# Two linear-attention and feed-forward layers on one core: down weights loaded behind small memsets, and a new order of the work

## The chip, the cores and the metric

The kernel runs on one core of a Trainium2 chip. The metric is device time in microseconds (us) of one execution; less is better. A core has five engines with an instruction queue each: TensorE (PE, matrix products), VectorE (DVE), ScalarE (ACT), GpSimd (POOL) and SyncE (SP, which here issues nearly all transfers). They run side by side and wait for each other by semaphores. Transfers are carried out by 16 DMA engines.

## The reference

x has 2048 rows of 512 columns. Two layers, one after the other, are applied twice, with the same weights:

```python
x = x + A(layernorm(x))      # 32 heads of 16, 4 segments of 512 rows
x = x + B(layernorm(x))      # gelu(x @ w_gate) * (x @ w_up) @ w_down, 1792 wide
# A, for segment s of a head:
p = softmax(q @ k.T * scale + causal_mask)         # within the segment
a_mem = (phi(q) @ M) / (phi(q) @ z + 1e-6)         # memory of earlier segments
o = g * a_mem + (1 - g) * (p @ v);  M += phi(k).T @ v;  z += sum(phi(k))
# phi(t) = t + 1 where t > 0, else exp(t); the result is o @ wo
```

## The kernel before

The work is cut into eight pieces, k = 0 to 7: four segments of 512 rows in the first pass through the two layers, four in the second. For each, PE makes q and k (512 rows by 128 columns at a time, four products of 128 deep each), v, the scores (computed transposed, so keys lie on partitions), the products of the exponentials (`pt`) with v, the memory's update and its reading, the output product, then gate, up and down of the feed-forward layer. All weights stay in on-chip memory: `wg_sb` and `wu_sb` (4 tiles of 1792 columns) and `wd_sb` (14 tiles of 512).

Nearly all products are split in four: four matmuls with 32 output columns of the array each, which run side by side (`product`, L654). So one product of 512 columns is four weight loads and four matmuls, eight instructions. PE's queue has 27,448 instructions.

The order of the work on every engine is set by a planner that runs when the program is built. `Clocks` keeps a modelled time for PE and for each other engine; work that becomes ready is posted to an engine (`post`, L255) with the time from which it is ready and a slack, and `serve` (L271) hands out the job with the earliest ready time plus slack. PE's products are items with a due time; at each step the main loop (at the end of the program) takes a step of scores if its exponentials have room, else the next ready item by due time. If there is no ready item but scores are still to come, it emits an unread product: a product of the constant tile `warm` into a free bank that nobody reads. The plan decides the order only; on the chip each engine works through its queue in that order and waits for real events. The table `CHANGES` alters the planner's slacks and due times each 8 us of modelled time.

ACT computes the exponentials (L1491), gelu (L1273) and some copies out of the accumulators; POOL masks the diagonal blocks of `pt` (L1464, `affine_select`) and makes `kS`, masked keys (L816); DVE does the rest. SP issues the weight loads (L498), the DMA transposes of normed rows and of phi(k) (L611: `xnT<-xn`, `phik<-e`), the copies of the odd heads' keys (L844: `kB<-kf`) and of half-segments' values (L888: `vS<-vaug`).

Weight loads are posted to SP from a list `pieces` of name, modelled time, size and a function that issues the load. The seven loads of the down weights (256 KB each) are the last of it: the first at `WD` = 40.3 us, then one each `WD_GAP` = 1.39 us. They have nothing to wait for but their place in SP's queue and the semaphores that DMA transfers share. The third part of x (`X3`, 512 KB) is such a piece too. At the start, PE runs `WARM` = 15 products of the whole array on the constant tile while the first rows of x are loaded and normed.

## Time and profile before

| | us |
|---|---|
| median of three runs | 557.79 (553.35 to 559.0) |
| the profiled execution | 553.77 |
| its span, first to last instruction | 552.0 |
| PE busy in it | 540.5 |
| mean granted clock of PE | 0.996 of full |

The profile is of one execution. The page gives busy times and groups of instructions; further views, which the prediction quotes, are the busy time by stretch (one row for each stretch of time; for each engine busy us and number of instructions, then the clock that PE was granted, the DMA engines' busy share and the GB/s that they moved), the waits (engine and line that waited, what it waited for, total us, number, longest), and the timeline (start, duration, engine, line, instruction, number merged into the row, and in brackets the idle time before it and what ended it). "issue" stands for idle time with no event that the profile shows. Durations of products overlap, since PE is pipelined: the step from one product to the next is shorter than the duration of one.

### The profile page before, as it was taken

Reading aid. Unit: us, or ns where it says so; the run is one execution under the profiler, and the core shown is the slowest. Engines: PE = TensorE matmul, PEld = TensorE weight load, DVE = VectorE, ACT = ScalarE, POOL = GpSimd, SP = SyncE. Lnnn points to the kernel's source line nnn. Section 1 sums busy time; section 2 is a strip of 40 time slices with the busy share of each in tenths; the row PEclk is TensorE's granted clock in tenths of the full one; section 3 lists DMA queues with packets and bytes.
Section 4 is the critical chain, followed back from the end, with each engine's and each line's share of the span. In section 5 each row is a group of like instructions: output and inputs, shape, how many; then the busy total and the mean of one; then the engine's idle time right before and its main releaser. Section 6 shows DMA issues by size and latency. Waiting matters only on the chain.

```text
span 552.0 us, 29935 instructions
## 1 busy us (share of the span) xinstructions
PE 540.5 (98%) x13723; PEld 296.2 (54%) x13723; DVE 434.6 (79%) x832; ACT 417.5 (76%) x391; POOL 242.2 (44%) x432
## 2 busy tenths in 40 slices
PE   8999899999999999999999999999999999999997
PEld 4446764765445444545444444555455455545994
DVE  7999599768996988689896976488989797587162
ACT  3899688989999877977989778947888865950600
POOL 6469044257538333924483345148593333121000
PEclk9999899999999999999999999999999999999999
DMA  8758515202500233301414020212254004100001
GB/s 254 188 130 173 127 34 98 34 4 55 96 13 4 37 48 60 51 2 33 60 33 60 14 41 4 50 33 41 42 89 71 4 8 94 13 12 32 14 5 41
DMA packets 69775, 30.39 MB, mean 55 GB/s; under 512 B 55120, under 2 KB 69200, under 8 KB 69648
## 3 DMA queue, kind: packets, MB, share of 16 engines
q1 hardware_dynamic: 69504, 28.46, 26.8%
q8 instruction: 107, 1.75, 1.4%
q14 instruction: 20, 0.16, 0.1%
q10 hardware_dynamic: 144, 0.01, 0.0%
HBM read 9.71 MB, written 2.10 MB: 21 GB/s over the span
## 4 chain that ended last, share of the span: by engine, by line
PE 89%; DVE 5%; ACT 2%; issue 1%; DMA 1%; POOL 0%; ACTq 0%; SPq 0%; DVEq 0%
PE big L654 75%; PE big L1421 8%; PE big L1117 6%; ACT pt L1491 1%; DVE x_sb L1218 1%; DVE st L677 1%; DMA vS<-vaug 1%; DVE byq L1145 1%; DMA x_sb<-in_A_x_dram 1%; DVE xn L713 0%; DVE st L1505 0%; POOL rs L1509 0%; DVE e L948 0%; DVE kS L816 0%; DVE ab L1153 0%
## 5 line engine op out<-in xcount | busy, mean ns | idle before, releaser
L1491 ACT ACTIVATE pt<-big 128x2048 bf16<-128x2048 f32 (+1 forms) x158 | 273.5, 1740 | 74.1 <-PE big L1421 68.1
L1464 POOL TENSOR_SCALAR_AFFINE_SELECT pt<-pt 64x256 bf16<-64x256 bf16 (+4 forms) x318 | 157.3, 522 | 227.1 <-ACT pt L1491 225.7
L1308 DVE TENSOR_TENSOR gel<-gel,big 128x512 bf16<-128x512 bf16 x112 | 74.9, 681 | 42.3 <-PE big L654 34.8
L654 PE MATMUL big<-xnT,wu_sb 128*32 128x512 bf16 (+1 forms) x2240 | 106.4, 339 | 0.5 <-issue 0.5
L654 PE MATMUL big<-xnT,wg_sb 128*32 128x512 bf16 (+1 forms) x2240 | 106.0, 337 | 0.0
L654 PE MATMUL big<-wd_sb,gel 128*32 128x512 bf16 (+2 forms) x1848 | 105.7, 373 | 0.0
L654 PEld LDWEIGHTS <-wu_sb 128*32 128x32 bf16 x2240 | 58.4, 97 | 35.1 <-issue 4.6
L654 PEld LDWEIGHTS <-wg_sb 128*32 128x32 bf16 x2240 | 57.9, 97 | 34.9 <-issue 5.4
L654 PEld LDWEIGHTS <-gel 128*32 128x32 bf16 x1848 | 46.7, 97 | 43.6 <-issue 4.6
L1218 DVE TENSOR_TENSOR x_sb<-x_sb,big 128x512 bf16<-128x512 bf16 (+1 forms) x65 | 43.1, 667 | 29.5 <-PE big L654 29.4
L1145 DVE STREAM_TRANSPOSE byq<-big 128x512 f32<-128x512 f32 x64 | 45.1, 705 | 12.5 <-PE big L1117 12.0
L1117 PE MATMUL big<-pt,vaug 128*32 128x64 bf16 (+5 forms) x1152 | 45.0, 263 | 2.4 <-issue 2.4
L677 DVE BATCH_NORM_STATS2 st<-x_sb 128x6 f32<-128x512 bf16 x60 | 40.5, 675 | 0.5
L1273 ACT ACTIVATE gel<-big 128x512 bf16<-128x512 f32 x64 | 34.9, 604 | 3.9 <-PE big L654 3.9
L654 PE MATMUL big<-xnT,wq_sb 128*32 128x512 bf16 (+1 forms) x528 | 35.0, 374 | 0.2 <-DVE xnT L755 0.2
L654 PE MATMUL big<-xnT,wk_sb 128*32 128x512 bf16 (+2 forms) x528 | 34.4, 373 | 0.2
L654 PE MATMUL big<-wv_sb,xnT 128*32 128x512 bf16 x512 | 32.3, 380 | 0.0
L654 PE MATMUL big<-wo_sb,aT 128*32 128x512 bf16 x512 | 31.9, 380 | 0.0
L816 POOL TENSOR_SCALAR kS<-kf,maskA 128x256 bf16<-128x256 bf16 x28 | 29.2, 1043 | 3.9 <-PE big L1421 3.0
L713 DVE TENSOR_SCALAR xn<-x_sb,mv,rs 128x512 bf16<-128x512 bf16 x64 | 28.9, 499 | 1.7 <-POOL rs L1509 0.9
L1117 PE MATMUL big<-pt,vS 128*32 128x64 bf16 x960 | 28.4, 193 | 1.3 <-DMA vS<-vaug 1.3
L816 POOL TENSOR_SCALAR kS<-kf,maskB 128x256 bf16<-128x256 bf16 x28 | 29.5, 1054 | 0.3
(98 smaller groups left out, 644.0 us busy)
## 6 DMA issues: line engine op xcount, KB each, us to landing
vS<-vaug SPq DMA_DIRECT2D x16, 136.0 KB, 3.1
out_dram<-x_sb SPq DMA_DIRECT2D x15, 128.0 KB, 1.9
wg_sb<-in_B_w_gate_dram SPq DMA_DIRECT2D x8, 224.0 KB, 5.6
wu_sb<-in_B_w_up_dram SPq DMA_DIRECT2D x8, 224.0 KB, 3.9
kB<-kf SPq DMA_DIRECT2D x28, 64.0 KB, 2.8
wd_sb<-in_B_w_down_dram SPq DMA_DIRECT2D x7, 256.0 KB, 4.7
x_sb<-in_A_x_dram SPq DMA_DIRECT2D x3, 512.0 KB, 6.4
xnT<-xn SPq DMA_TRANSPOSE x48, 2.8
```

The costliest lines, as they stand in the source:

```text
L654: nc.tensor.matmul(out[r], lhsT=lhsT[:, r], rhs=rhs, start=start, stop=stop, tile_position=(0, 32 * c))
L677: nc.vector.bn_stats(out=self.st6[:, 0, :], in_=x_sb[:, self.tt0 + j, :])
L713: eng.tensor_scalar(out=xn[:], in0=x_sb[:, self.tt0 + j, :], scalar1=self.mv[:, j, 0:1], scalar2=self.rs[:, j, :], op0=ALU.subtract, op1=A ...
L816: eng.tensor_scalar(out=kS[:, b, :, :, u], in0=self.kf[:, b, :].rearrange("p (t h c) -> p t h c", h=2, c=Q)[:, :, 0, :], scalar1=(maskA, m ...
L1117: nc.tensor.matmul(ps()[32 * j:32 * j + 32, q0 + shift:q1 + shift], lhsT=va[:, ki, values_of(va, b, p, j)], rhs=step["pt"][:, j, c0:c0 + q ...
L1145: nc.vector.transpose(out=self.byq[:, c], in_=ps()[:])
L1218: ck.dve.post(ck.made(), slack, (0.683 - 0.00104 * (D - width), lambda: nc.vector.tensor_tensor(out=xt, in0=xt, in1=ps()[:, 0:width], op=A ...
L1273: return lambda: nc.scalar.activation(out=out(), in_=in_(), func=ACT.Gelu_apprx_tanh)
L1308: ck.dve.post(ck.made(), NORMAL, (0.683, lambda: nc.vector.tensor_tensor(out=hidden(g, h), in0=hidden(g, h), in1=banked(ps), op=ALU.mult), ...
L1421: nc.tensor.matmul(big[:, got[j], c0:c0 + q1 - q0], lhsT=lhsT, rhs=a.q[rows, b, q0:q1], start=True, stop=True, tile_position=(32 * j, 0))
L1464: nc.gpsimd.affine_select(out=v, in_=v, pattern=[[0, m], [by, size]], compare_op=ALU.is_ge, fill=0.0, base=by - 1, channel_multiplier=-1)
L1491: 0.172 + 0.000832 * width * len(banks_of), lambda g=g, st=st: nc.scalar.activation(out=pt[:, g, 0:width], in_=st, func=ACT.Exp, scale=SCA ...
```

## The change

Three things are edited. One warm product less is emitted at the start (`WARM` 15 to 14). The down weights are planned from 50.0 us on with steps of 2.2 (before 40.3004 and 1.3897); each load is now a pair: a memset by POOL of one partition's first column in the two tiles that the load will fill, posted to POOL at the planned time, and the load itself, posted to SP when the planner holds the memset for done. Since both write the tile, the load waits for the memset on the chip. And many numbers of `CHANGES` are others, which orders the work anew everywhere. Cut to its core:

```diff
-WARM = 15
+WARM = 14
-WG_GAP, WU_GAP, WD_GAP = 1.1751, 1.964, 1.3897
+WG_GAP, WU_GAP, WD_GAP = 1.1751, 1.964, 2.2
-WO, WG, X2, WU, X3, WD = 8.92, 8.8357, 9.3414, 26.0, 59.6338, 40.3004
+WO, WG, X2, WU, X3, WD = 8.92, 8.8357, 9.3414, 26.0, 59.6338, 50.0
...
     for h in range(7):
         r = slice(2 * h, 2 * h + 2)
-        pieces.append(("down", WD + WD_GAP * h, 256, lambda r=r: load(
-            wd_sb[:, r, :], B_w_down.rearrange("(ft p) n -> p ft n", p=P)[:, r, :])))
+        pieces.append(("down", WD + WD_GAP * h, 256, (
+            lambda r=r: nc.gpsimd.memset(wd_sb[0:1, r, 0:1], 0.0),
+            lambda r=r: load(wd_sb[:, r, :], B_w_down.rearrange("(ft p) n -> p ft n", p=P)[:, r, :]))))
...
-        ck.sp.post(at, PIECE_SLACK, (Load(0.57), piece, issued))
+        if name == "down":
+            ck.pool.post(at, NORMAL, (0.1, piece[0], lambda t, piece=piece, issued=issued: ck.sp.post(
+                t, NORMAL, (0.57, piece[1], issued))))
+        else:
+            ck.sp.post(at, PIECE_SLACK, (Load(0.57), piece, issued))
```

What this does to the queues is seen in the order of the instructions (line, instruction, out<-in, size, number in a row). First SP, from the last loads of up weights to the third part of x. Before:

```order
L844 DMA kB_132<-kf 16x2048 x4
L498 DMA wu_sb<-in_B_w_up_dram 128x896 x2
L498 DMA wd_sb<-in_B_w_down_dram 128x2x512
L611 DMA_TRANSPOSE phik<-e 128x4x128
L498 DMA wd_sb<-in_B_w_down_dram 128x2x512 x2
L611 DMA_TRANSPOSE phik<-e 128x4x128
L498 DMA wd_sb<-in_B_w_down_dram 128x2x512 x4
L611 DMA_TRANSPOSE phik<-e 128x4x128
L498 DMA x_sb<-in_A_x_dram 128x4x512
```

Now (lines have moved by one):

```order
L845 DMA kB_131<-kf 16x2048 x4
L612 DMA_TRANSPOSE xnT<-xn 128x4x128
L498 DMA wu_sb<-in_B_w_up_dram 128x896 x2
L612 DMA_TRANSPOSE phik<-e 128x4x128 x2
L498 DMA wd_sb<-in_B_w_down_dram 128x2x512
L612 DMA_TRANSPOSE phik<-e 128x4x128
L498 DMA wd_sb<-in_B_w_down_dram 128x2x512 x4
L498 DMA x_sb<-in_A_x_dram 128x4x512
L498 DMA wd_sb<-in_B_w_down_dram 128x2x512 x2
L612 DMA_TRANSPOSE phik<-e 128x4x128
```

Two transposes of e (`phik<-e`) now stand ahead of the first down load and one behind it; the third part of x goes between the fifth and the sixth. On POOL the end of the masked keys for the second segment and the masks behind them. Before:

```order
L816 TENSOR_SCALAR kS<-kf,maskA 128x256
L816 TENSOR_SCALAR kS<-kf,maskB 128x256
L1464 AFFINE_SELECT pt<-pt 64x4x64 x8
L694 TENSOR_SCALAR ve<-mv 128x4
L700 TENSOR_TENSOR rs<-ve,mhalf 128x4
```

Now:

```order
L817 TENSOR_SCALAR kS<-kf,maskA 128x256
L817 TENSOR_SCALAR kS<-kf,maskB 128x256
L526 MEMSET wd_sb 1x2
L1465 AFFINE_SELECT pt<-pt 64x4x64 x4
L526 MEMSET wd_sb 1x2 x6
L1465 AFFINE_SELECT pt<-pt 64x4x64 x10
L695 TENSOR_SCALAR ve<-mv 128x4
```

One memset stands ahead of four masks, which wait for ACT's exponential, and six follow them in a row. On PE, ahead of the first products of the second segment's exponentials with v, before:

```order
L654 MATMUL big<-warm 32x512
L654 LDWEIGHTS warm
L654 MATMUL big<-warm 32x512
L1117 LDWEIGHTS vaug_134
L1117 MATMUL big<-pt,vaug_134 32x448
```

Now:

```order
L655 MATMUL big<-wo_sb,aT 32x512
L655 LDWEIGHTS aT
L655 MATMUL big<-wo_sb,aT 32x512
L1118 LDWEIGHTS vaug_133
L1118 MATMUL big<-pt,vaug_133 32x448
```

Unread products give way to output products of the first segment here. Over the whole program the unread products behind the warm ones are 49 before (196 matmuls) and 42 now (168). Four of the 42 are new ahead of products of the first segment's exponentials with v (in place of a q product, which follows later); the 22 that stood at 92 us and later are 11 in all, of which seven now stand ahead of the down products. Up to the scores that follow the first segment's first 56 gate products (half of its rows), PE's queue is the same but for such exchanges; then 16 q and 16 k matmuls, the 64 of the memory's update (`vaug,phik`) and again 16 and 16 of q and k come first, where before 64 matmuls of up came ahead of the update and 72 behind it. The first down product moves from the 3576th to the 4190th instruction of PE's queue.

80 lines of the change are left out of this document (40 added, 40 removed).

## The prediction

> **What bounds the kernel now.** I read the shares of the page first, then the busy time by stretch, then what TensorE (PE) waited for.
>
> ```profile
> PE 540.5 (98%) x13723; PEld 296.2 (54%) x13723; DVE 434.6 (79%) x832; ACT 417.5 (76%) x391; POOL 242.2 (44%) x432
> ```
>
> PE is busy for 540.5 of 552.0 us, so the time is PE's list of products plus PE's gaps. The busy time by stretch (us of PE first; then weight loads, DVE, ACT, POOL; the granted clock is the third number from the end) tells where the gaps are.
>
> ```profile
> 40.00:60.00 20.00, 18.41 (x539) 12.30 (x531) 16.68 (x33) 19.43 (x22) 13.86 (x21) 1.00 0.96 188
> 60.00:80.00 20.00, 17.79 (x581) 13.47 (x585) 16.57 (x36) 13.85 (x13) 3.54 (x8) 0.91 0.14 37
> 80.00:100.00 20.00, 18.74 (x500) 9.57 (x492) 17.24 (x34) 16.56 (x14) 10.10 (x17) 1.00 0.50 90
> 160.00:180.00 20.00, 20.00 (x491) 10.19 (x490) 15.04 (x27) 18.63 (x21) 14.10 (x18) 1.00 0.04 9
> ```
>
> From 160 us to the tail PE has no gap. Between 40 and 100 us it lacks 1.6 + 2.2 + 1.3 us, and only there does the clock fall below full. That is where this change works. The waits of PE, by what ended them:
>
> ```profile
> PE big L1117 <- issue: 2.4, 1, 2.4
> PE big L1117 <- DMA vS<-vaug: 1.3, 1, 1.3
> PE big L1421 <- ACT pt L1491: 1.1, 3, 0.6
> PE big L654 <- issue: 0.5, 1, 0.5
> ```
>
> "issue" is a gap that no semaphore explains. In the timeline the two stand here:
>
> ```profile
> 61.09 0.29 PE L1117 MATMUL big<-pt,vaug 128*32 128x192 bf16 x5 [2.41 <-issue]
> 72.27 0.39 PE L654 MATMUL big<-xnT,wu_sb 128*32 128x256 bf16 x5 [0.51 <-issue]
> ```
>
> What PE lacks there is its own instructions. Up to the first gap 1246 products have begun, up to the second 1630:
>
> ```profile
> 0.00:60.50 60.50, 56.16 (x1246) 30.71 (x1246) 51.16 (x115) 48.02 (x53) 36.33 (x62) 1.00 0.79 190
> 0.00:72.10 72.10, 66.84 (x1630) 39.84 (x1630) 60.00 (x134) 54.65 (x58) 37.85 (x66) 0.98 0.69 167
> q8 instruction: 107, 1.75, 1.4%
> ```
>
> The difference is 384 products with as many weight loads, 768 instructions. The instruction queue moved 1.75 MB in 107 packets, 16.4 KB each; PE's 27,448 rows over 107 are 256.5. So PE is fed in pieces of 256 instructions, and 768 is three of them: both gaps lie on the border of a piece. When was each piece asked for, and when did it come? One piece is 128 products, so the borders before these gaps lie at 1118 and 1502 products; and the instruction queue's packets are found in the DMA view of the windows 58.60 to 58.80 and 69.80 to 70.00 us:
>
> ```profile
> 0.00:55.30 55.30, 52.78 (x1118) 27.73 (x1118) 49.19 (x113) 42.96 (x46) 36.33 (x62) 1.00 0.75 186
> 0.00:69.10 69.10, 64.18 (x1503) 37.70 (x1507) 57.07 (x128) 51.76 (x56) 36.33 (x62) 0.98 0.72 174
> q8 instruction: 1, 0.02, 35.8%
> q8 instruction: 1, 0.02, 29.2%
> ```
>
> From the packet until PE goes on (58.7 to 61.09, 69.9 to 72.27) it takes 2.4 us both times. From the border to the packet it takes 0.7 us in the second case (69.1 to 69.8) but 3.3 in the first (55.3 to 58.6). What fills that stretch is DMA traffic (the last two numbers of a row are the DMA engines' busy share and GB/s):
>
> ```profile
> 55.50:59.00 3.50, 3.18 (x129) 2.91 (x128) 1.77 (x3) 3.47 (x7) 0.00 (x0) 1.00 1.13 333
> 60.50:62.20 1.70, 1.11 (x36) 0.79 (x40) 0.71 (x1) 0.40 (x1) 0.00 (x0) 1.00 1.02 303
> 62.50:66.50 4.00, 4.00 (x128) 3.64 (x124) 2.61 (x6) 2.46 (x2) 0.00 (x0) 0.57 0.03 8
> ```
>
> From 55.5 to 59.0 us the engines move 333 GB/s, and the packet got its turn at the end of that. SyncE's (SP) timeline says what it was:
>
> ```profile
> 51.11 1.20 SPq L611 DMA_TRANSPOSE phik<-e  x1
> 52.35 3.12 SPq L498 DMA_DIRECT2D wd_sb<-in_B_w_down_dram  x4
> 55.57 1.19 SPq L611 DMA_TRANSPOSE phik<-e  x1
> 56.81 0.59 SPq L498 DMA_DIRECT2D x_sb<-in_A_x_dram  x1
> ```
>
> Four loads of down weights, 1 MB, were posted at once. The gap of 2.41 us has a second price: one and a half us after it the clock falls, and 62.5 to 66.5 us runs at 0.57. That loses 4.00 x 0.43 = 1.72 us. The stall costs 4.13 us in all.
>
> **The change, part by part.** *One warm product less.* Behind the warm products PE waits for DVE's first normed rows (three short waits, 0.2 us at most), so the product's time becomes a longer wait. Zero; were the rows there earlier, one product of some 0.2 us would be won.
>
> ```profile
> PE big L752 <- DVE xn L713: 0.6, 3, 0.2
> ```
>
>
> *The memsets.* None on such a tile is in the trace; the nearest is GpSimd's (POOL's) memset of 4 columns.
>
> ```profile
> 0.79 0.10 POOL L557 MEMSET mhalf<- 128x4 f32 x1 [0.29 <-POOLq L1669]
> 51.96 2.25 POOL L1464 TENSOR_SCALAR_AFFINE_SELECT pt<-pt 64x256 bf16<-64x256 bf16 x4
> 70.46 0.79 POOL L1464 TENSOR_SCALAR_AFFINE_SELECT pt<-pt 64x256 bf16<-64x256 bf16 x2 [16.25 <-ACT pt L1491]
> 54.41 0.69 DVE L948 SCALAR_TENSOR_TENSOR e<-kf,e 128x512 bf16<-128x512 bf16 x1
> ```
>
> Seven of 0.10 us are 0.7 us on POOL, which has 16.25 us of idle time right behind them; without that cover they would delay the masks by 0.7. Their order decides more: one memset ahead of the masks at 51.96 and six in a row behind them, none waiting for anything. So the first load is held to about 52.0, and the other six are all free at about 54.2 + 0.7 = 54.9. They are held back, but not held apart.
>
> *When the loads run.* In SP's new order the first down load is followed by the transpose of e (ready when DVE ends at 55.1), then four down loads, x's third part, two down loads. SP's transpose takes 1.2 us, so the four are posted from 56.3 on. In the old run data moved 55.5 - 52.35 = 3.1 us after the first of four was posted: estimate 59.4 us for the new burst, then 1 MB in 3.1 us (to 62.5), with the other 1 MB to 65.7. Behind the waiting loads on SP stand only that transpose, x's part, the next segment's transposes and its kB; what needs the first is the memory update's products, whose rows now begin near 60.7 us. The transpose would land at 55.1 + 2.9 = 58.0 (median of its kind, below), so there are 2.7 us of cover; if POOL were later than SP by more than that, PE would wait for the rest.
>
> ```profile
> phik<-e SPq DMA_TRANSPOSE x24, 2.9
> vS<-vaug SPq DMA_DIRECT2D x16, 136.0 KB, 3.1
> 91.41 1.40 SPq L888 DMA_DIRECT2D vS<-vaug  x2
> ```
>
> *The fetch.* PE's rows up to the first gap are the same but for four unread products in place of a q product, equal in length. The border at 55.3 then finds one load on the engines rather than four; with the 0.7 and 2.4 us of the second gap its piece is there at 58.4, and PE needs it at 58.5. So the 2.41 and the 1.72 us go. What is late next is the following piece, asked for at 58.5 and on the engines at 59.2, while the new burst comes at 59.4. PE needs it after 5 + 8 small products (0.54 us, 61.09 to 61.63), 32 products of 512 columns, 64 of the update and 20 more of 512. The rows for those:
>
> ```profile
> 46.40 1.05 PE L654 MATMUL big<-xnT,wk_sb 128*32 128x512 bf16 x16
> 47.27 1.04 PE L654 MATMUL big<-xnT,wq_sb 128*32 128x512 bf16 x16
> 115.55 1.04 PE L654 MATMUL big<-vaug,phik 128*32 128x128 bf16 x56
> 116.52 0.41 PE L1421 MATMUL big<-q,kS 32*128 32x64 bf16 x32
> ```
>
> Sixteen of 512 take 0.87 us, 56 of the update 0.97. That is 0.54 + 1.74 + 1.11 + 1.09 = 4.5, so need at 63.0. If the fetch goes ahead of the burst it is there at 61.6: no gap. If it stands behind the four loads: 62.5 + 2.4 - 63.0 = 1.9 us. If behind all: 65.7 + 2.4 - 63.0 = 5.1. I take zero, because 59.2 is before 59.4, but 0.2 us is little. The 0.51 us gap stays: it belongs to a piece with 64 tiny products, which the new order also has in one piece.
>
> *The unread products.* The old order has 49 between its real products, the new one 42. Four took:
>
> ```profile
> 92.56 1.04 PE L654 MATMUL big<-warm 128*32 128x512 bf16 x16
> 93.43 0.36 PE L1117 MATMUL big<-pt,vaug 128*32 128x448 bf16 x4
> 95.05 0.21 PE L1117 MATMUL big<-pt,vS 128*32 128x64 bf16 x4 [1.26 <-DMA vS<-vaug]
> ```
>
> 0.87 us, 0.217 each; seven are 1.52 us. Every other product of PE is there in the same number, and changes between the two tilings of the array go from 294 to 295. The same rows show the wait for vS. In the new order SP issues that copy ahead of the segment's norm transposes, and PE has some 64 products of v and 32 of wo (96 x 0.054 = 5.2 us) between the last reader of the old vS and the first of the new, against 1.4 + 3.1 = 4.5 us of issue and landing (rows above). So 1.26 goes, though with 0.7 us of cover only. The ACT waits (1.1 in all) I leave as they are: without them the sum falls by 1.1, and as many new ones would add 1.1.
>
> *Sum.* The profiled execution took 553.77 us, 1.77 around its span of 552.0. 552.0 - 2.41 - 1.72 - 1.52 - 1.26 = 545.1, so 546.9. Three further runs took 559.0, 557.79 and 553.35; with the profiled one their mean is 556.0, 2.2 above it. I carry that over: **549.1, say 549**, against the median of 557.79.
>
> **Rivals.** *The stall moves* to the next piece: the burst is posted as one, and 0.2 us decide. Behind four loads 1.9 us, nearer to the 2.41 that cost the clock than to the 1.26 that did not, so with 1.72: 549.1 + 3.6 = 552.7. Behind all: 549.1 + 6.8 = 555.9.
>
> *Loads don't hold a fetch.* Then the first gap has another cause that this change leaves alone: 549.1 + 4.13 = 553.2. The page "DMA: Bandwidth & Descriptors" of the Trainium skill (Queues, rings and completion order) says each DMA engine takes turns between its queues packet by packet, by which a fetch would wait for one packet and not for a megabyte, and "Runtime: NRT & Kernel Launch" (Instruction fetch mechanics) calls the cost of a border mostly hidden. The trace agrees with that section's blocks of 256 instructions, but its 3.3 against 0.7 us from border to packet speaks against both rules here, hence a small chance.
>
> *Slower.* Where the old order has unread products and copies' waits, 75 to 98 us, the new one puts up and down products that wait for DVE's gel products. DVE is the busiest engine there after PE (16.57 and 17.24 of 20 us). If it lags by over 2.4 us at two places, each costs a gap and a fallen clock like the one at 58.6: 2 x 4.13 = 8.3, so 557.4 (555.2 on the profiled scale, above 553.77). Against it: the old order packs DVE as fully, and PE's waits for its xn, above, are of 0.2 us.
>
> **How the numbers follow.** Forecast 0.45, moved stall 0.28 (mostly at 552.7), loads without effect 0.10, slower 0.17. Low end: the forecast without the 0.51 and 1.1 us and without the carried 2.2 is 545.3, so 545. High end: the moved stall behind all loads and most of the slower case, 557. About one percent is what a measurement can tell: under 552.2 is faster. The forecast and a quarter of the moved cases (a fetch that waits for one or two of the loads) give 0.52 faster. Slower than 563.4 needs four such places instead of two (549 + 4 x 4.13 = 565.5), 0.08. The rest, 0.40, lies within one percent.
>
> **What would show it.** Right: no "issue" gap over 1 us near 58 to 66 us, clock 1.00 in every stretch of 20 us up to 540, the down loads posted between 52 and 60 us, no vS wait near 90. Moved: an "issue" gap 256 instructions later, near 63 us, with a clock below full behind it. Wrong: the gap where it was although one load at most ran beside its fetch; or PE waiting for DVE or ACT behind 160 us, where it never waited.

## The result, and the profile after

Beside each other on one chip, twenty executions each, the change took **553.09 us** in the median (550.28 to 558.34) and the kernel before 557.16 (553.34 to 561.19): ratio 0.994, 95% interval 0.9914 to 0.9967. A second comparison, below, gave 0.9964 (0.993 to 0.9998). So it is faster, by 0.4 to 0.6%, where 549 us (1.5%) was forecast. The profiled execution took 553.75 us with a span of 552.0, the same span as before's.

The shares first, then the busy time by stretch of the changed kernel, in the columns of before:

```profile
PE 538.8 (98%) x13694; PEld 294.1 (53%) x13694; DVE 438.7 (79%) x836; ACT 414.8 (75%) x376; POOL 233.8 (42%) x417
```

```profile
40.00:60.00 20.00, 19.10 (x572) 13.13 (x572) 16.26 (x34) 18.90 (x22) 14.62 (x28) 1.00 0.54 109
60.00:80.00 20.00, 17.19 (x616) 12.65 (x612) 17.66 (x37) 14.87 (x12) 3.05 (x8) 1.00 0.46 123
80.00:100.00 20.00, 18.11 (x482) 9.02 (x472) 18.80 (x38) 17.95 (x16) 10.56 (x19) 1.00 0.51 81
160.00:180.00 20.00, 20.00 (x488) 10.23 (x484) 16.39 (x26) 19.08 (x21) 13.90 (x16) 1.00 0.01 4
```

The clock is full up to 540 us, and 40 to 60 us has 0.7 us more of PE. But 60 to 80 lacks 2.8 us (2.2 before) and 80 to 100 lacks 1.9 (1.3 before). What PE waited for, from the waits:

```profile
PE big L655 <- issue: 2.3, 3, 1.7
PE big L655 <- DMA xnT<-xn: 2.0, 2, 1.2
PE big L1422 <- ACT pt L1492: 1.0, 2, 0.7
PE big L655 <- DVE am L1004: 0.9, 1, 0.9
PE big L1118 <- DVE xnT L646: 0.7, 1, 0.7
PE big L1118 <- issue: 0.2, 1, 0.2
```

The wait for vS is gone and ACT's 1.0 us is there as it was; the xnT, `am` and second xnT rows are new. In the timeline the larger gaps stand here:

```profile
47.46 1.05 PE L655 MATMUL big<-xnT,wq_sb 128*32 128x512 bf16 x16 [0.86 <-DMA xnT<-xn]
64.16 0.83 PE L655 MATMUL big<-xnT,wk_sb 128*32 128x512 bf16 x12 [0.35 <-issue]
68.71 1.39 PE L655 MATMUL big<-xnT,wu_sb 128*32 128x256 bf16 x44 [1.75 <-issue]
72.44 0.52 PE L1118 MATMUL big<-pt,vaug 128*32 128x256 bf16 x16 [0.20 <-issue]
98.83 1.05 PE L655 MATMUL big<-xnT,wq_sb 128*32 128x512 bf16 x16 [1.16 <-DMA xnT<-xn]
```

The border at 59.3 us, the one of the old stall, has no gap. Each of the next four has one (0.35, 1.75, 0.20 and, at 76.17, 0.22 us). SP's and POOL's timelines show the loads and the memsets that let them go:

```profile
52.65 0.39 SPq L498 DMA_DIRECT2D wd_sb<-in_B_w_down_dram  x1
55.89 1.20 SPq L612 DMA_TRANSPOSE phik<-e  x1
57.18 2.73 SPq L498 DMA_DIRECT2D wd_sb<-in_B_w_down_dram  x4
59.97 0.46 SPq L498 DMA_DIRECT2D x_sb<-in_A_x_dram  x1
60.54 1.32 SPq L498 DMA_DIRECT2D wd_sb<-in_B_w_down_dram  x2
```

```profile
52.51 0.10 POOL L526 MEMSET wd_sb<- 1x2 bf16 x1
54.98 0.25 POOL L526 MEMSET wd_sb<- 1x2 bf16 x6
```

Six memsets in a row, free at 55.2, and the loads in one burst behind the transpose at 55.89, as the queues had it.

### The profile page after: what moved, and what is told of

Same layout as the page of the kernel before. It is cut to its first block, busy times and chain, and to the rows that moved or that the text cites. A ratio compares the mean times of both kernels' runs of the same rounds, so it can differ in the third digit from the quotient of the medians.

```text
span 552.0 us, 29849 instructions
## 1 busy us (share of the span) xinstructions
PE 538.8 (98%) x13694; PEld 294.1 (53%) x13694; DVE 438.7 (79%) x836; ACT 414.8 (75%) x376; POOL 233.8 (42%) x417
## 3 DMA queue, kind: packets, MB, share of 16 engines
q8 instruction: 107, 1.75, 1.3%
## 4 chain that ended last, share of the span: by engine, by line
PE 79%; DVE 11%; DMA 3%; ACT 2%; issue 2%; POOL 2%; ACTq 0%; DVEq 0%; POOLq 0%
PE big L655 67%; PE big L1422 7%; PE big L1118 5%; ACT pt L1492 2%; DVE st L678 2%; DVE xn L714 1%; DVE x_sb L1219 1%; DMA xnT<-xn 1%; DVE byq L1146 1%; DVE e L949 1%; DMA amT<-am 1%; DMA phik<-e 1%; DVE ab L1154 1%; DMA x_sb<-in_A_x_dram 1%; POOL pt L1465 1%
## 5 line engine op out<-in xcount | busy, mean ns | idle before, releaser
L1465 POOL TENSOR_SCALAR_AFFINE_SELECT pt<-pt 64x256 bf16<-64x256 bf16 (+4 forms) x296 | 146.1, 520 | 238.8 <-ACT pt L1492 235.7
L655 PEld LDWEIGHTS <-wg_sb 128*32 128x32 bf16 x2240 | 57.7, 97 | 35.6 <-issue 6.1
L817 POOL TENSOR_SCALAR kS<-kf,maskA 128x256 bf16<-128x256 bf16 x28 | 30.4, 1085 | 3.5 <-PE big L1422 2.6
```

Source lines behind the costliest of these rows:

```text
L655: nc.tensor.matmul(out[r], lhsT=lhsT[:, r], rhs=rhs, start=start, stop=stop, tile_position=(0, 32 * c))
L817: eng.tensor_scalar(out=kS[:, b, :, :, u], in0=self.kf[:, b, :].rearrange("p (t h c) -> p t h c", h=2, c=Q)[:, :, 0, :], scalar1=(maskA, m ...
L1465: nc.gpsimd.affine_select(out=v, in_=v, pattern=[[0, m], [by, size]], compare_op=ALU.is_ge, fill=0.0, base=by - 1, channel_multiplier=-1)
```

## The experiments

The theory to begin with: a piece of PE's instructions is held by a burst of weight loads, so the stall went with the burst and came back where the burst now stands. The rival: the gaps belong to places in PE's order. Ratios are to the kernel before, executed beside each kernel; five rounds unless said otherwise. In all runs with an "untouched order" the other queues hold the same instructions in the same order.

**1. The old order with late loads.** Each down load now stands behind a DVE memset of its tile, and these behind the first seven gel products.

```diff
+    def let_go():
+        if later:
+            r = later.pop(0)
+            nc.vector.memset(wd_sb[0:1, r, 0:1], 0.0)
+            load(wd_sb[:, r, :], B_w_down.rearrange("(ft p) n -> p ft n", p=P)[:, r, :])
...
-        pieces.append(("down", WD + WD_GAP * h, 256, lambda r=r: load(
-            wd_sb[:, r, :], B_w_down.rearrange("(ft p) n -> p ft n", p=P)[:, r, :])))
+        pieces.append(("down", WD + WD_GAP * h, 256, lambda r=r: later.append(r)))
...
-                        out=hidden(g, h), in0=hidden(g, h), in1=banked(ps), op=ALU.mult),
+                        out=hidden(g, h), in0=hidden(g, h), in1=banked(ps), op=ALU.mult), let_go()),
```

> The kernel before with PE's order of work untouched; only the seven loads of down weights start later, one at a time: each waits for a DVE memset of its tile that stands behind one of the first seven gel products, so from about 63 us on. Theory (instruction pieces wait behind a burst of weight loads): the fetch of the piece asked for at 55.3 us finds the DMA engines nearly empty, so the 2.41 us 'issue' gap at 61.09 us and the half clock from 62.5 to 66.5 us (1.72 us) both go: 4.1 us less than before, ratio about 0.993. One load at a time (256 KB, some 0.8 us) holds a later fetch by no more than that, so later gaps stay at 0.5 us or below. Rival (the gap belongs to this place in PE's order and not to the loads): the 2.41 us gap stays near 61 us with its half clock, ratio 1.00.

554.94 us, 0.9959 (0.9932 to 0.9986). The stall at 61.09 is gone. In its place:

```profile
59.69 0.29 PE L1124 MATMUL big<-pt,vaug 128*32 128x256 bf16 x4 [1.40 <-ACT gel L1280]
64.04 0.42 PE L661 MATMUL big<-vaug,phik 128*32 128x128 bf16 x13 [0.38 <-issue]
69.14 1.05 PE L661 MATMUL big<-xnT,wu_sb 128*32 128x256 bf16 x29 [1.51 <-issue]
71.01 0.65 PE L661 MATMUL big<-zcols,phiq 128*32 128x8 bf16 x64 [0.82 <-DVE zcols L1066]
```

The loads do hold the fetch: without them its packet came at 56.1, 0.4 us behind the border. What they hid comes out: a wait for ACT's gelu, and a late piece at 69.14, whose fetch was asked for at 64.0 and came at 66.7 beside the third part of x and the first loads. The half clock, too, only moved: it stands at 71.3 us, for 3.4 us.

**2. The old order with a larger burst** (three rounds).

```diff
+    again = cst.tile([P, 2, D], BF16, name="again")
+    twice = {3: (x_sb[:, 12:14, :],), 4: (x_sb[:, 14:16, :],), 5: (again[:],)}
...
+        pieces.append(("down", WD + WD_GAP * h, 256, lambda r=r, h=h: [load(
+            dst, B_w_down.rearrange("(ft p) n -> p ft n", p=P)[:, r, :]) for dst in (
+                wd_sb[:, r, :],) + twice.get(h, ())]))
```

> The kernel before with a larger burst: three of the last four down loads are issued twice, the second time to places that nobody reads (the part of x_sb that its third part of x overwrites later, and a spare tile); 1.75 MB in one burst in place of 1 MB, PE's order untouched. Theory (the fetch of a piece waits until the burst is through): at 333 GB/s the burst takes 5.4 us in place of 3.1, so the instruction packet that came at 58.7 us comes near 61.0, and PE's gap of 2.41 us grows to about 4.7 us, again with the half clock behind it: 2.3 us slower than before, ratio 1.004. Rival (the gap is a fixed cost of that border, or the fetch takes turns with the loads): gap 2.4 us as before, ratio 1.00.

In the profile nearly as expected: the packet came at 61.4 us (4.4 us behind a border that PE itself reached 1.5 us later, in place of 3.2 to 3.4), and the gap grew to 3.78, with 0.86 more one border ahead:

```profile
56.98 2.58 PE L657 MATMUL big<-xnT,wg_sb 128*32 128x256 bf16 x85 [0.86 <-issue]
64.00 0.29 PE L1120 MATMUL big<-pt,vaug 128*32 128x192 bf16 x5 [3.78 <-issue]
```

Yet the median is 555.18, ratio 1.0001 (0.9967 to 1.0035): 2.2 us more of stall in the profile, and no longer on the whole. The profiled execution was the longest of the ten (560.73 us, with two half clocks), so its stall need not be that of the others; whether they had less of it, or got it back further on, is not shown.

**3. The new order with the old places of the loads.** Here `down_loads(n)` issues the next n of the seven loads; the memsets are left out.

```diff
+                    sb[:, kt, c], w_view(w)[:, kt, c]), n == "up" and ups.append(1), len(ups) == 8 and down_loads(1))))
...
-        ck.sp.post(t, slack, (1.3, lambda: nc.sync.dma_start_transpose(out=out(), in_=in_()), told))
+        ck.sp.post(t, slack, (1.3, lambda: (nc.sync.dma_start_transpose(out=out(), in_=in_()),
+                                  len(ups) == 8 and down_loads(2 if len(rest) == 6 else 4)), told))
```

> The changed kernel with PE's new order untouched; only the down loads go back to the places on SP's queue that they had before (one behind the last up load, two behind the next transpose of e, four behind the one after that), without memsets. Theory (pieces wait behind the burst): the stall of 2 to 2.4 us comes back at the border that the old one stood at (PE near 58 to 61 us), with a half clock behind it, 4.1 us in all; the two later gaps of 0.35 and 1.75 us at 64.16 and 68.71 us fall to 0.5 us or none, since the loads are through by then. Net about 2.5 us slower than the changed kernel: ratio to the kernel before 0.998 to 1.000 where the changed kernel has 0.994. Rival (the new order, not the loads, removed the old stall and made the new gaps): gap at 64 and 68.7 us stays, none near 58 to 61 us, ratio 0.994.

552.98 us, 0.9963 (0.9936 to 0.999), no different from the change. A gap of 1.17 us came back at 59.26 us, 1.60 followed at 64.08 (behind the third part of x), then 0.36, 0.47 and 0.22: 3.8 us in all and no half clock, where the theory had a stall of 2 to 2.4 us with a half clock, and no more than 0.5 behind it. PE was 2.7 us late already, by a wait at 49.29, so the stall itself was less. Where the loads stand decides at which border PE waits; the sum did not fall.

**4. The change without memsets.**

```diff
-            lambda r=r: nc.gpsimd.memset(wd_sb[0:1, r, 0:1], 0.0),
+            lambda r=r: None,
```

> The changed kernel without the seven memsets on GpSimd; every queue else keeps its order, so the loads are held only by their place on SP's queue. Theory (the memsets pace nothing, since six of the seven stand in a row and SP gets to the loads later than GpSimd does): loads posted at the same times within 0.5 us, the same burst from about 59.5 to 66.5 us, the same gaps, ratio 0.994. Rival (the memsets do hold the loads): loads start earlier by over 1 us, and the stall near 59 us comes back with its half clock, ratio 1.00.

555.32 us, 0.9981 (0.9951 to 1.0011). The first load was posted at 50.44 in place of 52.65, the six others from 56.8 to 61.2, within 0.7 us of before. So the memsets pace one load of seven. In this profile a gap came back at the old border, as the rival had it but with a full clock, and "issue" is 4.5 us from 59 to 75 us (2.5 and 3.3 in the two profiles of the change). The packet behind that gap came at 57.7, 2.0 us behind its border. No load was on the engines then, only a transpose of e, as the second row shows (share and GB/s at its end):

```profile
60.02 0.21 PE L1118 MATMUL big<-pt,vaug 128*32 128x64 bf16 x4 [1.05 <-issue]
```

```profile
55.75:57.70 1.95, 1.95 (x80) 1.95 (x75) 1.51 (x2) 1.92 (x3) 0.00 (x0) 1.00 1.22 63
```

So a transpose can hold a fetch too, and the earlier load is not shown to be the cause. The interval overlaps that of the change; whether that one load makes the difference of the medians is not settled.

**5. The new order, loads spread.** The edit of run 1 on the changed kernel.

> The changed kernel with PE's new order untouched; the down loads come one at a time, each behind a DVE memset of its tile that stands behind one of the first seven gel products, instead of six in one burst. Theory (the burst from 59.5 to 66.5 us holds the fetches behind the gaps of 0.35 us at 64.16 and 1.75 us at 68.71): both shrink, in sum from 2.1 to 0.5 us or less, and the clock has less cause to fall in the executions where it does: ratio 0.989 to 0.991. Rival (these gaps belong to PE's new order): they stay, ratio 0.994.

555.28 us, 0.9996 (0.9971 to 1.002): missed. The "issue" gaps moved to 70.54 (0.93 us) and 79.09 (1.59), in sum the 2.5 of the change. The loads were later than meant, and not one at a time: the first was posted at 70.56, and three stood together at 73.09, beside the fetch behind the gap at 79.09. The profiled execution also waited 2.54 us for xnT at 48.95, and its clock fell twice (49.2 and 79.9).

**6. The new wait at 47 us.** In the new order the transpose xnT stands on SP behind four kB copies.

Here the first four copies wait in a list until the next transpose has been issued.

```diff
-                        ck.sp.post(max(t, ck.pe), tn.KB_SLACK, (0.55, lambda r=r: nc.sync.dma_start(
-                            out=self.kB[r], in_=self.kf[r]), lambda t2: ck.at(t2 + 1.8, lambda: landed(t2 + 2.0))))
+                        ck.sp.post(max(t, ck.pe), tn.KB_SLACK, (0.55, lambda r=r: behind_turn(lambda: nc.sync.dma_start(
+                            out=self.kB[r], in_=self.kf[r])), lambda t2: ck.at(t2 + 1.8, lambda: landed(t2 + 2.0))))
...
+        ck.sp.post(t, slack, (1.3, lambda: (nc.sync.dma_start_transpose(out=out(), in_=in_()), let_copies_go()), told))
```

> The changed kernel with one exchange on SP's queue: the transpose xnT that the q product at 47.46 us waits for goes ahead of the four kB copies of 3.2 us in place of behind them, where the kernel before had it too; every other queue untouched. Theory (where the expected gain went: this place of the new order costs 0.86 us in the changed kernel's profile and 0.8 to 2.7 us in three other runs of its order, by how long the transpose takes to land): the wait is gone, 0.9 to 2.7 us less than the changed kernel, ratio to before 0.989 to 0.992. Rival (PE only comes sooner to the next thing that is late, a fetch or ACT's gelu near 59 us): the wait is gone but later gaps grow by as much, ratio 0.994.

552.56 us, 0.9955 (0.9937 to 0.9973). The wait is gone and the time is not: PE comes a microsecond sooner to the same late pieces (0.17, 0.36, 1.75, 0.20 us at 58.46 to 71.56). The rival's case.

**7. Loads out of the way.** As run 6, and the seven down loads go behind the third and the fifth up load.

```diff
+        for _ in range({3: 4, 5: 3}.get(len(ups), 0)):
+            r = rest.pop(0)
+            load(wd_sb[:, r, :], B_w_down.rearrange("(ft p) n -> p ft n", p=P)[:, r, :])
```

> As the run before, and the seven down loads are moved from 52-61 us into two idle stretches of SP near 30 us (four) and 35 us (three), where PE's pieces of 256 instructions last 5.5 to 6 us and a fetch has time to wait; no memsets, other queues untouched. Theory (what is left of the loss is fetches held by the burst, in a stretch where a piece lasts 3 to 4 us): no 'issue' gap over 0.6 us from 50 to 80 us but for one behind the third part of x, and no half clock there; 2 us less than the run before, ratio 0.985 to 0.989. Rival (the DMA engines' work is only moved, and the transposes of 28 to 47 us land later): PE waits for xnT or phik between 30 and 48 us, ratio 0.994 or above.

552.17 us, 0.9954 (0.9937 to 0.9971): nothing more than run 6, and here the theory fell. The gaps stand, and the fetches behind the second and the third had no load beside them. (The rival's sign is there as well: PE waited 0.99 us for xnT at 47.36, so a part of what the free engines brought was lost there.) PE's timeline, and two stretches between one late border and the next (the DMA engines' share and GB/s at the end of a row):

```profile
64.47 0.83 PE L675 MATMUL big<-xnT,wk_sb 128*32 128x512 bf16 x12 [0.36 <-issue]
...
66.45 0.69 PE L675 MATMUL big<-zcols,phiq 128*32 128x8 bf16 x64
...
68.47 1.39 PE L675 MATMUL big<-xnT,wu_sb 128*32 128x256 bf16 x44 [1.20 <-issue]
...
72.47 0.52 PE L1138 MATMUL big<-pt,vaug 128*32 128x256 bf16 x16 [0.47 <-issue]
```

```profile
62.40:65.60 3.20, 2.84 (x93) 1.83 (x85) 2.51 (x7) 2.83 (x3) 0.00 (x0) 1.00 0.00 0
64.40:68.47 4.07, 2.81 (x129) 2.01 (x128) 3.41 (x10) 2.97 (x4) 0.18 (x1) 1.00 0.02 4
```

From 64.4 to 68.47 us PE has 2.81 us of work in its 128 products, 64 of them of 8 columns, and waits for the rest of the time, though the engines move nothing but the fetch itself. From late border to late border it is 4.00 us both times. That the gaps belong to the borders holds for all 19 profiles: of their 55 "issue" gaps over 0.15 us behind 11 us, each has the same number of PE's instructions ahead of it, but for multiples of 256 and at most 17. Put together, border by border (packets to 0.2 us, from the DMA view in short windows):

| kernel | PE at the border | packet | PE goes on | gap | beside the fetch |
|---|---|---|---|---|---|
| before | 55.3 | 58.7 | 61.09 | 2.41 | burst |
| before | 69.1 | 69.9 | 72.27 | 0.51 | - |
| run 2 | 56.98, late | 61.4 | 64.00 | 3.78 | larger burst |
| change | 59.3 | 61.7 | 64.16 | 0.35 | burst |
| change | 64.16, late | 66.3 | 68.71 | 1.75 | rest of it |
| change | 68.71, late | 69.8 | 72.44 | 0.20 | - |
| run 7 | 59.5 | 62.2 | 64.47 | 0.36 | third part of x |
| run 7 | 64.47, late | 65.6 | 68.47 | 1.20 | - |
| run 7 | 68.47, late | 69.5 | 72.47 | 0.47 | - |

From a border that PE reaches late to the next late one it is 3.7 to 4.0 us with idle DMA engines; a burst adds up to 3 us. This is no fixed time: behind 72.47 in run 7 the next border, 3.5 us on, has no gap. The new theory: near 58 to 76 us PE has too many instructions for its work, so pieces with 2.8 to 3.5 us of work follow each other faster than they can be fetched, and what one gap loses the next need not.

**8. The old order, loads out of the way.** The edit of run 7's loads on the kernel before, behind the third and the fourth up load.

> The kernel before with PE's order untouched and the down loads moved to SP's idle stretch near 30 us (four) and 35 us (three). Theory (the old stall was the burst's; loads alone bring most of what the change brings): no 'issue' gap near 58 to 61 us, no half clock behind it; what appears beneath is ACT's gelu, 0.2 to 1.4 us; the 0.51 us gap at the piece with the 64 small products stays. 2.4 + 0.9 (half clock, as a mean) less what appears: ratio 0.994 to 0.997. Rival (the transposes near 35 to 45 us land later behind the loads): waits for xnT before 50 us, ratio 1.00.

557.29 us, 1.0001 (0.9971 to 1.0031): the stall gone, nothing gained.

```profile
45.54 1.05 PE L661 MATMUL big<-xnT,wq_sb 128*32 128x512 bf16 x16 [1.45 <-DMA xnT<-xn]
64.54 0.41 PE L661 MATMUL big<-vaug,phik 128*32 128x128 bf16 x13 [1.73 <-issue]
71.99 0.39 PE L661 MATMUL big<-xnT,wu_sb 128*32 128x256 bf16 x5 [1.26 <-issue]
```

"issue" is 3.1 us here and 2.9 in the kernel before: as much, further back. The rival's sign is there too, a wait for xnT at 45.54 that the profile of before has not; the run does not part the two. And the half clock of before probably had a use that I did not see: from 62.6 to 66.0 us it stretched the work behind the stall. The next packet came at 62.7, good for about 65.1 by the 2.4 us from packet to PE; PE reached that border at 65.4, and would have at 63.7 without the 1.7 us of half clock. That is an estimate from these figures; no run shows it.

**9. Fewer instructions.** On run 7: the memory's updates for the first two segments, and the second segment's reading of it, as products of the whole array.

```diff
+    def whole(k, out, lhsT, rhs, start=True, stop=True):
+        if k != 1:
+            return product(out, lhsT, rhs, start, stop)
+        ck.tiling("columns")
+        nc.tensor.matmul(out, lhsT=lhsT, rhs=rhs, start=start, stop=stop)
...
-                product(den()[:, j, b, :], self.phiq[:, b, j * P:(j + 1) * P], mem_state[k - 1][1][:, b, :])
+                whole(k, den()[:, j, b, :], self.phiq[:, b, j * P:(j + 1) * P], mem_state[k - 1][1][:, b, :])
...
-                product(psm()[:, b, :], self.phik[:, j, b * P:(b + 1) * P],
+                whole(k or 1, psm()[:, b, :], self.phik[:, j, b * P:(b + 1) * P],
```

> As the run with the loads at 30 and 35 us, and 384 instructions fewer on PE near 60 to 120 us: the memory's two first updates and the second segment's reading of it (z and the memory proper) are made by whole-array products, two instructions each, in place of four of 32 columns with eight. The same sums; order of the rest untouched. Theory (in this stretch PE is bound by its instructions: one late border follows the other by 3.7 to 4.0 us even where the DMA engines are idle, 64.47, 68.47 and 72.47 us in that run, and a piece with 64 products of 8 columns holds only 2.8 us of work): the 'issue' gaps of 0.36, 1.20, 0.47 and 0.61 us, 2.6 in all between 60 and 120 us, fall below 1.0; the products take the same time (128 columns about 0.06 us each by the first segment's transposes, 0.97 us for sixteen split ones) but those of 8 columns 0.4 us more; 1.2 to 2 us less, ratio to before 0.992 to 0.9935. Rival (the gaps belong to these places for another reason, or weight loads of the whole array are not hidden): gaps as before or PE 2 us longer, ratio 0.996 to 0.999.

**550.41 us, 0.9895 (0.9863 to 0.9927)**, by the ratio more than expected (3.3 us less than run 7; by the medians, which stem from two comparisons, 1.8), and all six executions between 549.35 and 550.64. Of the four "issue" gaps none is left; these are all that the timeline has from 11 to 140 us:

```profile
58.63 0.29 PE L1145 MATMUL big<-pt,vaug 128*32 128x256 bf16 x4 [0.76 <-ACT gel L1301]
75.72 0.40 PE L1449 MATMUL big<-q,kf 16*128 16x64 bf16 x8 [0.36 <-ACT pt L1519]
95.26 0.40 PE L1449 MATMUL big<-q,kB 32*128 32x64 bf16 x8 [0.73 <-ACT pt L1519]
```

The two profiled spans, 551.8 and 548.9 us, differ by 2.9: run 7 had 2.6 of "issue" and 0.99 of xnT at 47.36, run 9 has neither, but 0.55 more of gelu. The edit has nothing to do with that wait for xnT, so a part of the gain is not its own. And the products take no longer than those that they replace. In run 7, then in run 9 (start, us):

```profile
61.85 1.17 PE L675 MATMUL big<-vaug,phik 128*32 128x128 bf16 x64
66.45 0.69 PE L675 MATMUL big<-zcols,phiq 128*32 128x8 bf16 x64
```

```profile
61.72 1.14 PE L682 MATMUL big<-vaug,phik 128*128 128x128 bf16 x16
65.95 0.55 PE L682 MATMUL big<-zcols,phiq 128*128 128x8 bf16 x16
```

**10. Numbers alone, loads alone, and the change again** (loads alone three rounds). The planner plans anew in the first two.

```diff
-WG_GAP, WU_GAP, WD_GAP = 1.1751, 1.964, 2.2
+WG_GAP, WU_GAP, WD_GAP = 1.1751, 1.964, 1.3897
...
-WO, WG, X2, WU, X3, WD = 8.92, 8.8357, 9.3414, 26.0, 59.6338, 50.0
+WO, WG, X2, WU, X3, WD = 8.92, 8.8357, 9.3414, 26.0, 59.6338, 40.3004
```

> The changed kernel's numbers of the planner and its 14 warm products with the loads of the kernel before (planned from 40.3 us, no memsets). The planner makes another order of it, with 69 unread products in place of 42, 5.9 us more of PE. Theory (the numbers are fitted to the planned times of the loads, and the order counts by its unread products and its waits): the old burst and its stall near 58 to 61 us are back, 5.9 + 2 to 4 us above the changed kernel, ratio 1.005 to 1.015. Rival (unread products stand where PE would wait anyway, so they cost nothing): ratio 0.994 to 1.00.

569.81 us, 1.0283 (1.0249 to 1.0318), above what was expected. The profiled span is 13.0 us longer than the change's: 27 unread products more are 5.9 of it and waits 5.3, such as these; the rest is not accounted for:

```profile
PE big L1421 <- ACT pt L1491: 4.2, 7, 1.9
PE big L654 <- DMA xnT<-xn: 3.4, 3, 2.3
```

> The change's loads (planned from 50.0 us in steps of 2.2, with memsets) with the numbers of the planner and the 15 warm products of before. The planner makes another order of it, with 58 unread products in place of 49 (2.0 us). Theory (the planner's numbers are fitted to one set of loads, as the run with the numbers alone showed): new waits as there, ratio 1.005 to 1.02. Rival (the numbers bring nothing, the loads everything): 2.0 - 2.4 - 0.9 = -1.3 us, ratio 0.998.

567.81 us, 1.0201 (1.0156 to 1.0246), the upper end. Neither half of the change stands without the other where the planner plans anew. That the numbers were fitted to one set of loads, in the old pair as in the new, agrees with both runs; as the order changes with them, they do not show it alone.

> The changed kernel as it is, beside the others on one chip, for a second profile of it. Theory (its gaps at 64 and 68 us are the instruction pieces', at fixed places; its waits for xnT near 47 and 98 us depend on how long a transpose takes to land): 'issue' gaps from 60 to 76 us between 2.0 and 3.6 us in all at the same borders; the xnT waits anywhere from 0 to 2.7 us each; ratio 0.992 to 0.997. Rival (all of them vary alike): 'issue' gaps below 1 us or above 5.

554.67 us, 0.9964 (0.993 to 0.9998). "issue" 3.3 us between 60 and 76 us, xnT 0.63 and 1.38: as expected. It is one gap of 2.85 at 68.96 and one of 0.47 at 72.96 this time.

**11. Which decides, the burst or the number?** The function of run 9 on three other kernels: the change with its burst, the kernel before, and run 8.

> The changed kernel, its loads and memsets untouched, with the 384 instructions fewer on PE (whole-array products for the memory's first two updates and the second segment's reading of it). Theory (PE's instructions per us decide in this stretch, the burst only where a piece is short): the 'issue' gaps from 60 to 76 us, 2.5 us in the first and 3.3 us in the second profile of the changed kernel, fall below 1.0 us although the burst still stands beside the fetch asked for near 59 us; 1.5 to 2.5 us less than the changed kernel, ratio to before 0.990 to 0.993. Rival (the burst decides, and the last run owed its gain to the early loads): a gap of 1.5 us or more stays between 62 and 70 us, ratio 0.994 to 0.996.

550.03 us, 0.9895 (0.9868 to 0.9923): the same as with the loads out of the way. The profiled span is 3.6 us shorter than the change's; 1.8 of it is "issue", and 1.16 the wait for xnT at 98.83, which this profile has not, as those of runs 7 and 9 have not. The one "issue" gap from 11 to 140 us lies at the border ahead, whose packet came at 57.1, before the burst:

```profile
47.49 1.05 PE L655 MATMUL big<-xnT,wq_sb 128*32 128x512 bf16 x16 [0.90 <-DMA xnT<-xn]
60.08 0.21 PE L1125 MATMUL big<-pt,vaug 128*32 128x64 bf16 x4 [0.74 <-issue]
```

The next piece's packet came at 62.9, 2.8 us behind the border and inside the burst, and nothing waited for it, because the piece at 60.08 now holds 6.1 us of work:

```profile
60.00:66.20 6.20, 6.12 (x132) 3.57 (x131) 5.36 (x12) 4.95 (x5) 0.00 (x0) 1.00 1.02 302
```

> The kernel before, its loads and order untouched, with the same 384 instructions fewer. The first instruction left out comes behind the stall at 61.09 us. Theory: that stall of 2 to 2.5 us stays, since the piece before it is as full as it was and its fetch stands behind the burst; the gaps behind it (0.51 us at 72 us) go; ratio 0.997 to 0.999. Rival (the number of instructions alone decides): the stall at 61 us goes too, ratio 0.993 to 0.995.

555.11 us, 0.9984 (0.9963 to 1.0006), and as expected the stall ahead of the first product left out stays (1.63 us at 60.32, here with a full clock behind it), while the gap near 72 is gone.

> The kernel before in its old order with the loads at 30 and 35 us (that run: 'issue' gaps of 1.73 us at 64.54 and 1.26 us at 71.99, ratio 1.000) and the 384 instructions fewer. Theory: the gap at 71.99 us goes; the one at 64.54 us stands ahead of the memory's update and stays, up to the 1.73 us that the third part of x gives it; 1.3 to 2 us less than that run, ratio 0.996 to 0.998. Rival (only the new order gains by it): ratio 1.000.

554.47 us, 0.9971 (0.9941 to 1.0001), as expected. "issue" is 0.7 us (0.38 of it at 65.22, none near 72), but the old order waited for vS in this profile:

```profile
93.85 0.25 PE L1131 MATMUL big<-pt,vS 128*32 128x64 bf16 x4 [2.07 <-DMA vS<-vaug]
```

**12. Everywhere, and the best version.** Run 11's first kernel with whole-array products in all segments; and the same kernel (second segment only) with run 6's exchange.

```diff
-        if k != 1:
+        if not k:
```

> The run with the changed kernel's own loads and 384 instructions fewer, now with whole-array products for every update and every reading of the memory: 1,728 instructions fewer than the changed kernel. Theory (only where a piece of 256 instructions holds less than 4 us of work does their number count, and behind 160 us PE has no 'issue' gap): no further gain, ratio to before 0.988 to 0.991. Rival (fewer instructions help everywhere): 1,344 more of them at 0.016 us (4.0 us for 256), 21 us: ratio 0.95 to 0.96; or split products are quicker where nothing starves: 0.993 or above.

551.35 us, 0.9918 (0.9889 to 0.9946), between the theory's range and the rival's: 1,344 instructions fewer gain nothing where no piece is late. The interval overlaps that of run 11's first kernel, so whether they cost anything is not settled.

> The same run (384 instructions fewer, loads in their burst) with the transpose xnT ahead of the four kB copies on SP's queue. Theory (the 0.9 us wait at 47.49 us is on PE's path, and no fetch behind it takes the gain now): 0.5 to 1 us less, ratio 0.987 to 0.989. Rival (PE meets ACT's gelu or the fetch near 59 us sooner and waits there): the wait is gone, ratio 0.9895 unchanged.

**549.07 us, 0.9874 (0.9836 to 0.9911)**, all six executions between 548.58 and 549.41: faster than both kernels. The profile has neither the wait at 47 us nor an "issue" gap. So the exchange that gained nothing in run 6 seems to be worth its microsecond now (550.03 to 549.07, though the two intervals overlap).

## Why the direction was right and the size wrong

Term by term, of the 552.0 us span (the right column from the two profiles of the change, run 10's in brackets, but for the half clock, which is from the means below):

| term | forecast | found |
|---|---|---|
| stall at 61.09 | -2.41 | -2.4 |
| half clock | -1.72 | -0.1 |
| unread products (rows of 12.7 and 11.6 us) | -1.52 | -1.1 |
| wait for vS | -1.26 | -1.3 |
| next pieces, from 0.51 | 0 | +2.0 (+2.8) |
| other new waits | 0, at most 1.1 | +3.8 (+3.7) |

**The step that failed** is "I take zero, because 59.2 is before 59.4" for the piece after the stall. It failed twice over. PE reached that border at 59.3 in place of 58.5, by the new wait of 0.86 us at 47.46, and the burst began at 59.4 as estimated. (Run 6, without that wait, reached it at 58.5, but its burst began then too, and the gap was 0.36.) So the fetch stood in the burst, as the rival "the stall moves" had it, but behind 0.6 of its 2 MB: its packet came at 61.7 and the gap was 0.35, not 1.9, with no half clock. That the 553.1 us measured lie near that rival's 552.7 is luck, for they are made of other parts. And with the burst away (run 7) 2.0 us of gaps stayed. My working compared one fetch with one need; it did not ask how much work lies in the pieces *behind*. The piece at 64 us has 64 products of 8 columns and 2.8 us of work in the profile, less than the 0.7 + 2.4 us that I had myself worked out for a fetch, and 3.7 to 4.0 where PE reaches the border late. I had the tiny products in view for the 0.51 us gap ("which the new order also has in one piece") and left it at 0.51. For the same reason my signs failed: all of "Right" but the loads' last 2 us came true (no gap over 1 us up to 66 us, a full clock, no vS wait), as the gap of 1.75 us stands at 68.71, one border behind the place that I watched.

**The new waits** are the larger miss by size: I put them at nothing and bounded them at 1.1 us by ACT's row, which does not bear on them. They are xnT 2.0, `am` 0.9, xnT by DVE 0.7 and 0.2 for byq. The first of the two xnT waits (0.86 at 47.46) could be read ahead of the result: in SP's new order that transpose stands behind the four kB copies, in the old ahead of them, and the copies take 2.5 us of SP in before's timeline. I went past this row because the part on SP's queue followed the down loads only. What makes the second (1.16 at 98.83) is not shown. Of the rival "slower" these are the wrong waits (it had DVE's gel products) and too small to turn the sign.

**The half clock** was a term of one execution. Over the 120 executions of the kernel before that the later comparisons use, the granted clock's shortfall times the span is 0.95 us in the mean, 66 of them at 0.999 of full clock or above; over 32 of the change it is 0.85. So 0.1 us was to be had, not 1.72.

**The carried 2.2 us** fitted the kernel before and not the change. The 120 executions have a mean of 556.2, 2.5 above the profiled one; the 32 of the change have one of 553.9, 0.1 above theirs (553.75). The two profiled spans are the same, 552.0, so the profiles do not show the gain at all. The found column is +0.9 us (-0.7 with the 1.7 of half clock that before's profile had, so 0.7 are not placed; run 10's profile comes to 0.0), the means differ by -2.4: the old order loses, as a rule, some 3.3 us that the one profile that I worked from did not lose. What these 3.3 us are stays open, since only one execution of the kernel before was profiled. Other kernels in the old order waited 0.9 to 3.2 us for vS and up to 2.8 for xnT in runs 1, 2, 8 and 11, against 1.3 and nothing in that profile, so waits of this kind are likely. The direction was right, then, but in part by luck: what went as forecast was eaten up by what came new, and the gain that was measured is of another making.

**Right** were: the cause of the first gap (run 1: without the loads beside it the packet came 0.4 us behind the border, and the stall was gone), its going, the place of the loads (posted from 52.65 to 61.86, where the sign had 52 to 60), six of them not held apart by the memsets (run 4), the vS wait, ACT's waits, and nearly no wait behind 160 us: 0.93 us for `am` at 415.33 and 0.18 at 457.74, which "Wrong" had named and which are small.

## What to carry to other kernels

Where a gap has no event behind it, count instructions: work per piece of 256 against the time from one late border to the next tells whether moving a transfer can help, or whether the stretch needs fewer instructions (here a quarter of them did the same products in the same time, and only there it paid). A stall taken away on a chain of late things is taken back by the next late thing until the chain itself is shorter; so look for what is late next over the whole stretch, not over one step. And price a change against several executions: a term that occurs in half of them is worth half.

## What the runs showed of the hardware

*The fetch of PE's instructions.* Unloaded, a border reached late was followed by the next late one after 3.7 to 4.0 us (1.1 us to the packet, 2.6 to 2.9 from there), and at times by one without a gap after 3.5 (run 7, 72.47 to 75.93). Behind 160 us, where pieces last some 5 us (392 us for 9,644 products of the change), the change had no "issue" gap; other kernels had single ones where a piece was short (1.12 us at 458.94 in run 10's first, 3.4 us behind the border ahead). The Trainium skill, "Runtime: NRT & Kernel Launch" (Instruction fetch mechanics), calls the crossing of a block mostly hidden; that holds here where a piece has over 4 us of work and the DMA engines are idle, and not where it has 2.8.

*The fetch beside transfers.* Its packet came 2.1 to 4.4 us after the border while loads ran (table above), and 2.0 us beside a transpose (run 4), against 0.4 to 1.1. By the Trainium skill, "DMA: Bandwidth & Descriptors" (Queues, rings and completion order), an engine takes turns between its queues packet by packet; run 2, in which with a longer burst the packet came 4.4 us behind its border in place of 3.2 to 3.4, speaks against that as the whole account.

*The clock.* Ahead of the tail a fall lasted 3.4 us whatever came ahead of it, and once, around a wait of 3.27 us in run 12's first kernel, 6.8. In before's profile, in run 11's third kernel behind a wait of 2.07 us, and, without a fall, in the second profile of the change around a wait of 2.85 us:

```profile
62.60:66.00 3.40, 3.40 (x104) 3.09 (x100) 2.14 (x5) 2.36 (x2) 0.00 (x0) 0.50 0.02 5
```

```profile
93.70:97.10 3.40, 3.25 (x56) 1.55 (x60) 1.67 (x4) 1.69 (x1) 0.00 (x0) 0.52 0.44 80
```

```profile
66.00:74.00 8.00, 4.68 (x176) 3.70 (x171) 5.55 (x12) 3.46 (x3) 1.53 (x4) 1.00 0.14 33
```

So 2.07 us cost a fall and 2.85 did not. In run 5 the clock fell behind a gap of 1.59 us (79.09), and in run 10's loads alone it did not behind one of 3.08 (509.96). So in these profiles the length of a wait alone does not decide. The Trainium skill, "TensorE: Matmul & The Clock Gate" (What's actually happening), tells of windows of 3.4 us that run free of the kernel; that agrees with the length, and would account for the rest.

*Executions.* The transposes xnT landed 2.4 to 4.6 us after their issue in both profiles of the change, and 2.4 to 4.7 in run 12's second kernel. Executions of the change differ by 8 us, while six of that kernel, which has neither late pieces nor the wait at 47 us, lie within 0.83 us. That waits for late transposes and falls of the clock make the difference is likely, and not shown, since most executions have no profile.
